# Seven block products for eight in the first FFN products of the last 768 tokens

## The chip, the cores and the metric

The kernel runs on one core of a Trainium2 chip. The metric is the device time of one execution in microseconds (us). One execution was also recorded by the hardware profiler; its own time stands in the table below. Engines are named as the profile names them: PE (TensorE, matmuls), PEld (its weight loads), DVE (VectorE), ACT (ScalarE), POOL (GpSimd), SP (the queue from which all DMAs of this kernel are issued).

## The reference

Attention over 4 batches of 8 heads (576 positions, head size 64) keeps only scores within `tau` of the row's maximum. Its output, 2304 tokens of 512 channels, runs through two feed-forward layers with 2048 hidden channels:

```python
scores = scale * np.matmul(q, k.transpose(0, 1, 3, 2))
thresh = np.max(scores, axis=-1, keepdims=True) - tau
attn   = softmax of the scores that are >= thresh, zero elsewhere
x = (attn @ v) as tokens x channels                      # 2304 x 512
h = x @ w_in;  g = np.maximum(h, 0.0) + alpha * np.minimum(h, 0.0);  x = g @ w_out      # layer 1
h = x @ w_in2; g = h * np.clip(h + 3.0, 0.0, 6.0) / 6.0;             out = g @ w_out2   # layer 2
```

The four weight matrices come as float64. In each FFN product both operands are split into a high and a low float32r part, and three matmuls (high by high, low by high, high by low) make one product.

## The kernel before

**Blocks and weights.** The 2304 tokens are cut into blocks 0 to 3 of 512 tokens (the first 512 positions of each batch) and block 4 of 256 (the last 64 positions of each batch). The hidden channels are 16 tiles of 128, each with one chunk of `w_in` (512 x 128) and one of `w_out` (128 x 512). Block 0's pass decodes each chunk from float64 (`decode`) and writes it to a scratch tensor in DRAM; every later pass loads it from there (`st`, 256 KB) and splits it again into `wi` or `wo` (`split`, L100 to L102: a cast on ACT, a subtraction on POOL or DVE).

**Attention and the queue.** Attention is emitted tile by tile at high priority. `ffn_groups` turns blocks 0 to 2, both layers, into 192 groups: an `h_group` computes one hidden tile (12 matmuls of 512 columns at L216, activation, split of `g`), an `o_group` adds four hidden tiles into one quarter of the output (12 matmuls at L246 or L252). The loop at the end takes groups from this queue between attention tiles at `per` groups a tile; the rest comes after attention.

**The tail.** Blocks 3 and 4 depend on the last attention tiles and run last, layer 1 and then layer 2. For each of 16 hidden tiles and each of the two blocks there are 12 matmuls at L216 (512 columns, then 256), the activation, the split of `g`, and two steps later the output product: L246 in layer 1 (12 of 512 and 12 of 256 columns), L252 in layer 2 (18 of 512 columns). The output sums of a whole layer stay in PSUM.

**What sets the order.** The text of the program, the priorities and a scheduler that simulates the engines fix the order of the instructions on each engine when the program is built. At run time each engine, and SP too, works strictly in that order: a DMA whose operand isn't ready holds every DMA behind it on SP. Tile pools give the buffers; a tile in a reused buffer waits for the last reader of the tile before it.

Of the kernel before, what the change touches and what calls it, by code (L numbers as in the profile page):

```python
# [32 lines left out]
def kernel(  # L33
# [46 lines left out]
    stage = pool(ctx, "stage", 4)  # L80
    gp = pool(ctx, "gp", 5)
    tmp = pool(ctx, "tmp", 2)
    wip = pool(ctx, "wip", 2)
    wop = pool(ctx, "wop", 5)
    dec = pool(ctx, "dec", 3)
    xp = pool(ctx, "xp", 1)
# [493 lines left out]
    x2p = pool(ctx, "x2p", 1, side="right")  # L580
# [5 lines left out]
    ps_h = pool(ctx, "ps_h", 2, space=PSUM)
    ps_o = pool(ctx, "ps_o", 1, space=PSUM)  # L590
    NBR = blocks[B]
    LAGO = 2
    xs = {blk: load_x(x2p.tile([P, 2, NKT, blocks[blk]], F32R, tag=f"x{blk}", name="x"), x1d[blk], blocks[blk], nc.vector)
          for blk in (B - 1, B)}
    for layer in (1, 2):
        c0 = passes.index((layer, None)) * NF
        ready("i", c0)
        oa = [ps_o.tile([P, SM], F32, tag=f"o{d}", name=f"o{d}") for d in range(4)]
        orr = [ps_o.tile([P, SM], F32, tag=f"r{d}", name=f"r{d}") for d in range(2)]
        gss, ys = {}, {}  # L600
        seq = [(ft, blk) for ft in range(NF) for blk in (B - 1, B)]
        for m in range(len(seq) + LAGO):
            if m < len(seq):
                ft, blk = seq[m]
                n = blocks[blk]
                h = ps_h.tile([P, SM], F32, tag="h", name="h")
                mm_h(h, ws["i", c0 + ft], xs[blk], n)
                g = act1(h, ft, n) if layer == 1 else act2(h, ft, n)
                gss[m] = g_hi(g, n)
                g_lo(gss[m], g, n)  # L610
                if blk == B - 1:
                    fetch("i", c0 + ft + 1)
                    ready("o", c0 + ft)
                    ready("i", c0 + ft + 1)
            if m < LAGO:
                continue
            ft, blk = seq[m - LAGO]
            gs = gss.pop(m - LAGO)
            n = blocks[blk]
            first_, last_ = ft == 0, ft == NF - 1  # L620
            if last_ and layer == 1:
                ys[blk] = x2p.tile([P, 2, NKT, n], F32R, tag=f"y{blk}", name="y")
            if layer == 1:
                for d in range(ND):
                    o = oa[d][:, 0:n] if blk < B else orr[d // 2][:, (d % 2) * 256:(d % 2) * 256 + n]
                    mm_o1(o, ws["o", c0 + ft], gs, d, n, first_, last_, fresh=blk < B or d % 2 == 0)
                    if last_:
                        split(ys[blk][:, 0, d], ys[blk][:, 1, d], o, nc.vector)
            else:
                for d in range((n + P - 1) // P):  # L630
                    o = oa[d] if blk < B else orr[d]
                    mm_o2(o, ws["o", c0 + ft], gs, d, n, first_, last_)
                    if last_:
                        t = ob.tile([P, SM], F32, tag="ob", name="ob")
                        w = min(P, n - d * P)
                        if d % 2:
                            nc.vector.tensor_scalar_mul(t[:w], o[:w], 1.0 / 6.0)
                        else:
                            nc.scalar.activation(t[:w], o[:w], AF.Copy, scale=1.0 / 6.0)
                        store(blk, d, t)  # L640
        xs = ys


# [29 lines left out]
```

## Time and profile before

| | us |
|---|---|
| median of three runs (lowest, highest) | 1180.61 (1177.13, 1181.27) |
| the profiled execution, own time | 1179.44 |
| its span, first to last instruction | 1177.7 |
| PE busy in the span | 1125.7 (96%) |
| tail: first matmul of layer 1 on block 3 or 4 to the last matmul | about 892 to 1172 |

The profile gives each engine's busy time, and idle time with what ended it. PE's busy time covers overlapping, modelled matmuls, so the length of one matmul is better taken from the start-to-start distance of a run of them: the chain of waits shows such runs with their start, length and count. A wait on PE costs time; a wait on another engine only if PE waits for it in turn.

### The profile page before, as it was taken

What the parts mean: (1) busy time and instruction counts of PE and PEld (TensorE: products, weight loads), DVE (VectorE), ACT (ScalarE), POOL (GpSimd) and SP (SyncE); (2) the same over time, 40 slices, a digit from 0 to 9 for tenths busy, and PEclk for the clock granted to TensorE, in tenths of its full rate; (3) what the DMA queues carried; (4) which work ended last, traced back from release to release, by engine and by line L of the source; (5) the groups of instructions that cost most, each with busy time, mean ns of one, the idle gap of its engine ahead of it and who ended that gap; (6) DMA issues with size and microseconds to landing.
All of it is one profiled execution on the core that took longest, in us unless ns stands there. A gap on an engine that the chain in (4) does not pass through costs nothing.

```text
span 1177.7 us, 19454 instructions
## 1 busy us (share of the span) xinstructions
PE 1125.7 (96%) x6944; PEld 934.1 (79%) x6944; DVE 649.2 (55%) x1295; ACT 662.6 (56%) x1272; POOL 674.3 (57%) x715
## 2 busy tenths in 40 slices
PE   5799999998999999999999999999999999999998
PEld 4677887777777888888887878887778888888886
DVE  6877798879697545555363537373236333331221
ACT  6887788777787656455655555455434222243332
POOL 2765689887788766555464755545334434334432
PEclk9799999999999999999999999999999999999999
DMA  5743266575766543242424432322235322222211
GB/s 166 218 128 82 80 201 211 152 235 177 230 205 194 149 118 97 76 129 72 124 73 114 137 95 73 103 76 69 83 90 157 86 63 63 63 63 63 64 37 54
DMA packets 92770, 137.51 MB, mean 117 GB/s; under 512 B 19328, under 2 KB 48512, under 8 KB 92672
## 3 DMA queue, kind: packets, MB, share of 16 engines
q1 hardware_dynamic: 92672, 136.26, 39.9%
q8 instruction: 55, 0.90, 0.3%
q14 instruction: 43, 0.35, 0.1%
HBM read 101.72 MB, written 25.17 MB: 108 GB/s over the span
## 4 chain that ended last, share of the span: by engine, by line
PE 71%; ACT 7%; DMA 6%; DVE 6%; issue 4%; POOL 4%; SPq 1%; ACTq 0%; POOLq 0%; DVEq 0%
PE h L216 26%; PE o L246 13%; PE o L252 13%; PE pv L442 5%; PE s L378 5%; PE t L424 3%; DMA st<-wo 2%; PE r L246 2%; PE r L252 2%; PE pt L323 1%; POOL wo L102 1%; DMA wo<-f 1%; ACT f L149 1%; ACT e L400 1%; DVE nmx L399 1%
## 5 line engine op out<-in xcount | busy, mean ns | idle before, releaser
L216 PE MATMUL h<-x,wi 128*128 128x512 f32 (+1 forms) x1536 | 354.4, 379 | 1.1 <-DVE acc L504 0.6
L242 POOL TENSOR_TENSOR gs<-g,gs 128x512 fp32r<-128x512 f32 (+1 forms) x160 | 191.1, 1194 | 216.9 <-ACT gs L238 216.0
L216 PEld LDWEIGHTS h<-x,wi 128*128 128x128 f32 x1536 | 272.3, 188 | 53.4 <-DVE acc L504 1.0
L252 PE MATMUL o<-wo,gs 128*128 128x512 f32 x768 | 195.3, 399 | 8.8 <-DVE g L232 4.7
L246 PE MATMUL o<-gs,wo 128*128 128x512 f32 x768 | 193.5, 397 | 6.2 <-DVE acc L504 2.2
L252 PEld LDWEIGHTS o<-wo,gs 128*128 128x128 f32 x768 | 141.3, 189 | 42.2 <-DVE g L232 7.1
L246 PEld LDWEIGHTS o<-gs,wo 128*128 128x128 f32 x768 | 139.9, 188 | 38.3 <-DVE g L224 5.0
L232 DVE SCALAR_TENSOR_TENSOR g<-m,h 128x512 f32<-128x512 f32 x80 | 50.5, 632 | 163.8 <-ACT m L230 162.3
L221 DVE TENSOR_SCALAR m<-h,alpha_sb 128x512 f32<-128x512 f32 x80 | 55.6, 695 | 148.9 <-PE h L216 148.6
L399 DVE TENSOR_REDUCE nmx<-s 128x1 f32<-128x576 f32 x144 | 107.6, 751 | 37.7 <-PE s L378 37.3
L400 ACT ACTIVATE e<-s,nmx 128x576 f32<-128x576 f32 x144 | 106.9, 747 | 37.4 <-DVE nmx L399 36.8
L238 ACT CAST gs<-g 128x512 fp32r<-128x512 f32 (+1 forms) x160 | 92.8, 580 | 62.3 <-DVE g L224 27.8
L411 POOL TENSOR_SCALAR e<-e,rc 128x576 f32<-128x576 f32 x144 | 109.0, 768 | 29.3 <-DVE rc L408 28.3
L402 DVE SCALAR_TENSOR_TENSOR e<-s,thr,e 128x576 f32<-128x576 f32 x144 | 116.0, 811 | 17.3 <-ACT e L400 14.4
L102 POOL TENSOR_TENSOR wi<-st,wi 128x512 fp32r<-128x512 f32 x56 | 72.9, 1302 | 78.4 <-ACT wi L101 78.2
L442 PE MATMUL pv<-p,v 128*64 128x128 f32 (+1 forms) x1600 | 108.9, 272 | 6.7 <-DVE g L224 2.2
L230 ACT ACTIVATE m<-h,three 128x512 f32<-128x512 f32 x80 | 51.5, 646 | 112.8 <-PE h L216 112.5
L101 ACT CAST wo<-st 128x512 fp32r<-128x512 f32 x96 | 57.1, 619 | 94.1 <-DMA st<-wo 78.2
L442 PEld LDWEIGHTS pv<-p,v 128*64 128x64 f32 x1600 | 84.1, 139 | 29.3 <-issue 16.4
L378 PE MATMUL s<-ka,qt 128*128 128x288 f32 x512 | 100.5, 323 | 6.2 <-DVE thr L401 3.6
L102 POOL TENSOR_TENSOR wo<-st,wo 128x512 fp32r<-128x512 f32 x56 | 74.3, 1343 | 50.9 <-ACT wo L101 50.9
L101 ACT CAST wi<-st 128x512 fp32r<-128x512 f32 x96 | 59.0, 615 | 78.2 <-PE h L216 41.5
(86 smaller groups left out, 1611.8 us busy)
## 6 DMA issues: line engine op xcount, KB each, us to landing
st<-wi SPq DMA_DIRECT2D x96, 256.0 KB, 2.7
st<-wo SPq DMA_DIRECT2D x96, 256.0 KB, 2.7
raw<-in_moe_w_in_dram SPq DMA_DIRECT2D x32, 512.0 KB, 4.6
raw<-in_moe_w_out_dram SPq DMA_DIRECT2D x32, 512.0 KB, 4.2
ka<-ka SPq DMA_DIRECT2D x30, 304.0 KB, 4.3
wi<-f SPq DMA_DIRECT2D x32, 256.0 KB, 3.8
wo<-f SPq DMA_DIRECT2D x32, 256.0 KB, 3.8
raw<-in_k_dram SPq DMA_DIRECT2D x16, 256.0 KB, 3.4
```

The lines of the kernel that those rows point to most:

```text
L101: nc.scalar.copy(hi, src)
L102: lo_eng.tensor_tensor(out=lo, in0=src, in1=f32(hi), op=ALU.subtract)
L216: nc.tensor.matmul(h[:, :n], lhsT=w[:, ws, kt * P:(kt + 1) * P], rhs=x[:, xs, kt, :n], start=(i == 0), stop=(i == len(steps) - 1))
L242: nc.gpsimd.tensor_tensor(out=gs[:, 1, :n], in0=g[:, :n], in1=f32(gs[:, 0, :n]), op=ALU.subtract)
L246: nc.tensor.matmul(o[:, :n], lhsT=w[:, ws, dt * P:(dt + 1) * P], rhs=gs[:, gsel, :n], start=fresh and start and i == 0, stop=stop and i == ...
L252: nc.tensor.matmul(o[:m, :], lhsT=gs[:, gsel, tt * P:tt * P + m], rhs=w[:, ws, :], start=start and i == 0, stop=stop and i == 2)
L378: nc.tensor.matmul(ps[:, half, 0:SH], lhsT=w, rhs=s["k"][:, a, c + half * SH:c + half * SH + SH], start=(n == 0), stop=(n == len(mms) - 1))
L399: nc.vector.tensor_reduce(out=nmx, in_=ps, axis=AX.XY, op=ALU.max, negate=True)
L400: nc.scalar.activation(eh, ps, AF.Exp, bias=nmx, scale=1.0)
L402: nc.vector.scalar_tensor_tensor(out=eh, in0=ps, scalar=thr, in1=eh, op0=ALU.is_ge, op1=ALU.mult, accum_out=sm[:, h:h + 1])
L411: nc.gpsimd.tensor_scalar(out=eh, in0=eh, scalar1=rc[:, h:h + 1], scalar2=0.0, op0=ALU.mult, op1=ALU.add)
L442: nc.tensor.matmul(pv[64 * h:64 * h + 64, :], lhsT=vn[:, h, kt, :], rhs=pt[:, blk, c:c + m], start=(kt == 0), stop=(kt == NB), skip_group_ ...
```

## The change

The tail is written anew. Blocks 3 and 4 are taken as one matrix of 768 tokens. Its product with `w_in` is cut in two along each of its three dimensions: two halves of 384 tokens, two halves of the 512 input channels (256 each), and hidden tile `i` beside hidden tile `i + 8`. Eight block products of 384 columns would make the two hidden tiles; seven make them from sums and differences of the blocks (`half1`, `half2`), at the cost of more additions. The output products keep their number, in another tiling (`o_tile`: 384 columns in layer 1, 512 in layer 2, over four hidden tiles, summed in SBUF).

- **Operands.** Four blocks of x and four differences (T1 to T4; B12 isn't needed itself) are made and split by `x_step`. The seven weight operands of a pair come by DMA, already split (`w_ready`, 1.84 MB, in a `whl` tile): three blocks from `parts`, four sums from `sums`.
- **`parts`.** In block 2's pass each split weight chunk, 64 of 512 KB, is also written to DRAM (in `ready`).
- **`sums`.** `block_sums` makes the four sums of a pair: two loads of 256 KB, four additions of 128x256 on POOL, four splits (ACT cast, POOL subtraction), four writes of 256 KB. Layer 1's eight jobs run between the queue's groups during blocks 1 and 2 (`run_group`); layer 2's eight run in the tail, one for each step of layer 1.
- **Pace.** Eight groups of the queue are kept for after attention (`TAIL`); the first two pairs' products are woven into the last five (`AHEAD`).
- The tail no longer loads and splits `wi` and `wo` chunks; it loads `w_out` split (`wo_ready`, 512 KB).

```diff
@@ ready: every split chunk of block 2 also goes to DRAM
             ws[kind, c] = w
+            if blk == B - 2:
+                nc.sync.dma_start(parts[nm, ft], f32(w))
@@ new
+    def block_sums(layer, i, wf_pool, sh_pool):
+        wf = wf_pool.tile([P, 4, 2 * P], F32, tag="wf", name="wf")
...
+        for out_, in0, in1, op, n in ((a22, a21, a22, ALU.add, 0), (a21, a11, a21, ALU.subtract, 2),
+                                      (a11, a22, a11, ALU.subtract, 1), (a12, a12, a11, ALU.subtract, 3)):
+            nc.gpsimd.tensor_tensor(out=out_, in0=in0, in1=in1, op=op)
+            sh = sh_pool.tile([P, 2, 2 * P], F32R, tag="sh", name="sh")
+            split(sh[:, 0], sh[:, 1], out_, nc.gpsimd)
+            nc.sync.dma_start(sums[layer, i][:, :, 2 * P * n:2 * P * n + 2 * P], f32(sh))
@@ queue
-    per = len(queue) / max(1, NS - PB)
+    jobs = [(1, i) for i in range(NF // 2)]
+    first = len(queue) // (B - 1)
+    every = (len(queue) - TAIL - first) // len(jobs)
...
+    per = (len(queue) - TAIL) / max(1, NS - PB - LAG)
@@ tail, new
+    def w_ready(layer, i):
...
+        w = (whl_q if i % 3 == 2 else whl_p).tile([P, 2, 7, KH], F32R, tag="whl", name="whl")
+        nc.sync.dma_start(f32(w[:, :, 1:3]), parts[f"i{layer}", i].rearrange("p a (b n) -> p a b n", b=2))
+        nc.sync.dma_start(f32(w[:, :, 3:7]), sums[layer, i].rearrange("p a (b n) -> p a b n", b=4))
+        nc.sync.dma_start(f32(w[:, :, 0]), parts[f"i{layer}", i + FH][:, :, KH:])
...
+    def prod(bank, w, x, first):
+        steps = [(ws_, xs_, kt) for ws_, xs_ in ((0, 0), (1, 0), (0, 1)) for kt in range(2)]
+        for n, (ws_, xs_, kt) in enumerate(steps):
+            nc.tensor.matmul(bank[:, 0:TN], lhsT=w[:, ws_, kt * P:kt * P + P], rhs=x[:, xs_, kt, :],
+                             start=first and n == 0, stop=n == len(steps) - 1, skip_group_check=True)
+
+    def half1(i, w, x):
...
+        prod(b1, w["A11"], x["B11"], True)
+        prod(b2, w["S2"], x["T2"], True)
+        prod(b3, w["S1"], x["T1"], True)
...
+        nc.scalar.copy(p1, c1)
+        nc.vector.tensor_tensor(out=u2, in0=c2, in1=p1, op=ALU.add)
+        prod(b1, w["A12"], x["B21"], False)
+        prod(b2, w["S3"], x["T3"], False)
+        nc.vector.tensor_tensor(out=hc[:, 2], in0=c2, in1=p1, op=ALU.add)
+        nc.vector.tensor_tensor(out=hc[:, 2], in0=c3, in1=hc[:, 2], op=ALU.add)
...
+    def half2(i, w, x, made):
+        prod(b2, w["A22"], x["T4"], False)
+        prod(b3, w["S4"], x["B22"], False)
+        nc.vector.tensor_tensor(out=hc[:, 1], in0=b2[:, 0:TN], in1=p1, op=ALU.add)
+        nc.vector.tensor_tensor(out=hc[:, 0], in0=b3[:, 0:TN], in1=u2, op=ALU.add)
...
+    whl_q = pool(rt, "whl3", 1)
+    wo_p = pool(rt, "wo2", 6)
+    gs_p = pool(rt, "gs2", 8)
+    sh_p = pool(rt, "sh2", 2)
```

On PE, in the middle of the tail's layer 1, this stood before (`h` is the first product, `o` and `r` the output sums of blocks 3 and 4):

```order
L216 MATMUL h<-x,wi 128x512 x12
L246 MATMUL o_10493<-gs,wo 128x512 x3
L246 MATMUL o_10494<-gs,wo 128x512 x3
L246 MATMUL o_10495<-gs,wo 128x512 x3
L246 MATMUL o_10496<-gs,wo 128x512 x3
L216 MATMUL h<-x,wi 128x256 x12
L246 MATMUL r_10497<-gs,wo 128x256 x6
L246 MATMUL r_10498<-gs,wo 128x256 x6
```

And this stands there now (`b` is a PSUM bank of block products of one pair, `xT`, `xB` the x operands, `gs` the split activations):

```order
L688 MATMUL b_11728<-xT_10733,whl 128x384 x2
L688 MATMUL b_11729<-xT_10728,whl 128x384 x6
L688 MATMUL b_11727<-xB_10744,whl 128x384 x6
L792 MATMUL o_11767<-gs_11505,wo_11390 128x384 x3
L792 MATMUL o_11767<-gs_11512,wo_11392 128x384 x3
L688 MATMUL b_11852<-xB_10723,whl 128x384 x3
L792 MATMUL o_11781<-gs_11505,wo_11390 128x384 x3
L688 MATMUL b_11728<-xT_10738,whl 128x384 x6
L792 MATMUL o_11781<-gs_11512,wo_11392 128x384 x3
```

The 24 products of one hidden tile have become 42 for a pair of hidden tiles, all of 384 columns, and products of two pairs stand woven with the output tiles of an earlier one.

On SP, at the end of attention, this stood before (`x1d` is the attention output in DRAM, written from `xo`):

```order
L453 DMA x1d_60<-xo 128x512
L169 DMA st<-wo_15_163 128x512
L454 DMA x1d_61<-xo 128x64
L209 DMA st<-x1d_60 128x512 x4
L209 DMA st<-x1d_61 128x256 x4
L169 DMA st<-wi_1_101 128x512
```

And this stands there now (`pi` is a weight chunk's copy in `parts`, `s` a pair's tensor in `sums`):

```order
L484 DMA x1d_60<-xo 128x512
L212 DMA pi_14_149<-wi 128x1024
L175 DMA st<-wi_0_183 128x512
L646 DMA whl<-pi_0_103 128x2x512
L485 DMA x1d_61<-xo 128x64
L647 DMA whl<-s_0_167 128x2x1024
L648 DMA whl<-pi_8_111 128x2x256
L646 DMA whl<-pi_1_104 128x2x512
L647 DMA whl<-s_1_168 128x2x1024
L648 DMA whl<-pi_9_112 128x2x256
L739 DMA xf<-x1d_60 128x4x512
L739 DMA xf<-x1d_61 128x4x256
```

The load of the tail's x (`xf`, 1.57 MB) now stands behind both `whl` tiles of the first two pairs.

On SP, near the end of the tail's layer 1 (nothing of the kind stood there before: a load of `st` for each chunk was all), now:

```order
L646 DMA whl<-pi_1_136 128x2x512
L647 DMA whl<-s_1_176 128x2x1024
L648 DMA whl<-pi_9_144 128x2x256
L234 DMA s_5_180<-sh 256x1x256 x2
L225 DMA wf<-wi_15_230 128x512
L225 DMA wf<-wi_7_222 128x512
L655 DMA wo_11825<-po_7_126 128x1024
L655 DMA wo_11827<-po_15_134 128x1024
L655 DMA wo_12160<-po_0_151 128x1024
```

The `w_out` tiles of layer 1's last pair (`wo_11825`, `wo_11827`) take the buffers of the pair three before, so their loads wait until that pair's last output product is done.

## Rows read from the trace of the kernel before

**Rows 1.** Page, busy time, share of the span and instructions of each engine

```profile
span 1177.7 us, 19454 instructions
PE 1125.7 (96%) x6944; PEld 934.1 (79%) x6944; DVE 649.2 (55%) x1295; ACT 662.6 (56%) x1272; POOL 674.3 (57%) x715
```

**Rows 2.** Windows: stretch, length, busy us by engine, granted TensorE clock, DMA

```profile
core 0: us, PE busy (x) PEld busy (x) DVE busy (x) ACT busy (x) POOL busy (x), PEclk, DMA share, GB/s
130.00:400.00 270.00, 255.34 (x1597) 209.19 (x1598) 224.12 (x434) 210.76 (x393) 223.89 (x228) 0.99 0.63 190
400.00:890.00 490.00, 481.27 (x2977) 396.64 (x2976) 238.19 (x472) 254.20 (x497) 267.35 (x276) 1.00 0.34 97
900.00:1036.00 136.00, 136.00 (x771) 118.94 (x770) 51.15 (x87) 38.27 (x70) 54.10 (x49) 1.00 0.29 81
1037.00:1172.00 135.00, 134.67 (x679) 113.48 (x677) 29.92 (x52) 51.56 (x99) 52.12 (x47) 1.00 0.17 47
```

**Rows 3.** Chain of waits inside the tail's layer 1: start, us, what

```profile
924.42 2.79 PE h L216 x12
927.21 2.75 PE o L246 x12
929.96 1.43 PE h L216 x12
931.38 1.43 PE r L246 x12
932.82 2.79 PE h L216 x12
```

**Rows 4.** Waits on PE from 400 to 890 us: total, times, longest

```profile
PE o L252 <- DVE g L232: 2.5, 6, 0.6
PE pv L442 <- DVE g L224: 2.2, 2, 1.6
```

**Rows 5.** Groups by form, whole span: busy us, mean ns of one, idle before

```profile
L242 POOL TENSOR_TENSOR gs<-g,gs 128x256 fp32r<-128x256 f32 x32 | 24.3, 760 | 36.4 <-ACT gs L238 36.4
L242 POOL TENSOR_TENSOR gs<-g,gs 128x512 fp32r<-128x512 f32 x128 | 166.8, 1303 | 180.5 <-ACT gs L238 179.6
L238 ACT CAST gs<-g 128x256 fp32r<-128x256 f32 x32 | 13.0, 407 | 12.6 <-PE o L252 5.6 <-DVE g L224 5.3 <-DVE g L232 1.1
L238 ACT CAST gs<-g 128x512 fp32r<-128x512 f32 x128 | 79.8, 623 | 49.7 <-DVE g L224 22.4 <-DVE g L232 13.8 <-PE o L252 7.1
L224 DVE SCALAR_TENSOR_TENSOR g<-h,m 128x256 f32<-128x256 f32 x16 | 6.8, 424 | 1.7
L504 DVE TENSOR_TENSOR acc<-o,acc 128x512 f32<-128x512 f32 x36 | 24.4, 683 | 25.6 <-PE o L246 25.6
```

**Rows 6.** Page, DMA issues: count, KB each, median us to landing

```profile
st<-wo SPq DMA_DIRECT2D x96, 256.0 KB, 2.7
raw<-in_moe_w_out_dram SPq DMA_DIRECT2D x32, 512.0 KB, 4.2
x1d<-xo SPq DMA_DIRECT2D x12, 256.0 KB, 3.1
```

**Rows 7.** DMA from 930 to 1030 us: queue, packets, MB, share of 16 engines

```profile
q1 hardware_dynamic: 3456, 6.29, 23.0%
```

**Rows 8.** DMA from 310 to 320 us: GB/s in 40 slices, and queue

```profile
GB/s 160 266 274 344 365 381 401 410 414 406 418 410 418 393 406 362 376 388 379 387 407 328 205 164 115 57 106 78 164 180 229 279 340 393 401 406 393 360 356 385
q1 hardware_dynamic: 2454, 3.15, 93.9%
```

**Rows 9.** Windows, the same columns as Rows 2, around that stretch

```profile
310.00:320.00 10.00, 7.90 (x47) 6.10 (x46) 4.14 (x6) 6.29 (x14) 4.99 (x6) 0.83 0.95 318
```

**Rows 10.** Timeline of PE between attention and tail: start, us, idle before

```profile
882.37 0.80 PE L442 MATMUL pv<-p,v 128*64 128x64 f32 x20
894.62 2.14 PE L216 MATMUL h<-x,wi 128*128 128x512 f32 x8 [0.37 <-ACT x L101]
```

**Rows 11.** Timeline of the last us of the span

```profile
1172.06 0.69 DVE L637 TENSOR_SCALAR ob<-r 128x512 f32<-128x512 f32 x1 [0.52 <-PE r L252]
1172.50 2.52 SPq L534 DMA_DIRECT2D out_dram<-ob  x4
```

More of the change, by code (lines that the diff above doesn't have):

```diff
@@ L62 @@
     LAG = 3
+    TAIL = 8
     OG = 4
@@ L79 @@
     const = pool(ctx, "const", 1)
[L80 to L86, printed above, removed]
+    mid = ExitStack()
+    wip = pool(mid, "wip", 2)
+    stage = pool(mid, "stage", 4)
+    wop = pool(mid, "wop", 5)
+    tmp = pool(mid, "tmp", 2)
+    gp = pool(mid, "gp", 5)
+    xp = pool(mid, "xp", 1)
+    decs = ExitStack()
+    rawp = pool(decs, "rawp", 1)
+    dec = pool(decs, "dec", 3)
     ident = const.tile([P, P], F32, name="ident")
@@ L107 @@
     scratch = {}
+    parts = {(nm, ft): dram.tile([P, 2, DM], F32, name=f"p{nm}_{ft}") for nm in weights for ft in range(NF)}
+    sums = {(layer, i): dram.tile([P, 2, DM * 2], F32, name=f"s{layer}_{i}") for layer in (1, 2) for i in range(NF // 2)}
     if wide:
@@ L204, in ready, with w_src @@
             ws[kind, c] = w
+            if blk == B - 2:
+                nc.sync.dma_start(parts[nm, ft], f32(w))
+    def w_src(nm, ft):
+        if wide:
+            return scratch[nm, ft]
+        return chunk(nm, ft)
+    def block_sums(layer, i, wf_pool, sh_pool):
+        wf = wf_pool.tile([P, 4, 2 * P], F32, tag="wf", name="wf")
+        for slot, ft in ((0, i + NF // 2), (2, i)):
+            src = w_src(f"i{layer}", ft)
+            dst = wf[:, slot:slot + 2]
+            if wide:
+                nc.sync.dma_start(dst.rearrange("p a n -> p (a n)"), src)
+            else:
+                nc.sync.dma_start(dst.rearrange("p a (k f) -> p (a k) f", k=2), src)
+        a21, a22, a11, a12 = [wf[:, s] for s in range(4)]
+        for out_, in0, in1, op, n in ((a22, a21, a22, ALU.add, 0), (a21, a11, a21, ALU.subtract, 2),
[4 more added lines that the diff above has]
+            nc.sync.dma_start(sums[layer, i][:, :, 2 * P * n:2 * P * n + 2 * P], f32(sh))
     def load_x(t, src, n, lo_eng):
@@ L264 @@
     ps_t = pool(psum, "ps_t", 2, space=PSUM)
-    ps_ho = pool(psum, "ps_ho", 2, space=PSUM)
+    ho_bank = ExitStack()
+    ps_ho = pool(ho_bank, "ps_ho", 2, space=PSUM, side="right")
     qr = []
@@ L539, with run_group @@
         queue += ffn_groups(1, b) + ffn_groups(2, b)
-    per = len(queue) / max(1, NS - PB)
+    jobs = [(1, i) for i in range(NF // 2)]
+    first = len(queue) // (B - 1)
+    every = (len(queue) - TAIL - first) // len(jobs)
+    cmb, cmbs = [], ExitStack()
+    def run_group(n):
+        f, a = queue[n]
+        f(*a)
+        if n == first - 1:
+            decs.close()
+            cmb.append(pool(cmbs, "cmb", 2))
+        if n >= first and (n - first) % every == every // 2 and jobs:
+            block_sums(*jobs.pop(0), cmb[0], cmb[0])
+            if not jobs:
+                cmbs.close()
+    per = (len(queue) - TAIL) / max(1, NS - PB - LAG)
+    qs_sb = const.tile([P, 1], F32, name="qs_sb")
+    ntau_sb = const.tile([P, 1], F32, name="ntau_sb")
     x0 = new_x()
@@ L575 @@
         while done < min(len(queue), (i + 1 - PB - LAG) * per):
-            f, a = queue[done]
-            f(*a)
+            run_group(done)
             done += 1
     att.close()
[L580 to L583, printed above, removed]
-    psum.close()
[L589 to L594, printed above, removed]
@@ L595 @@
-    for layer in (1, 2):
[L596 to L622, printed above, removed]
-            if layer == 1:
[L624 to L628, printed above, removed]
-            else:
[L630 to L641, printed above, removed]
@@ new lines @@
+    rt = ExitStack()
+    xop = pool(rt, "xop", 1, side="right")
+    xf_p = pool(rt, "xf", 1, side="right")
+    xt_p = pool(rt, "xt", 2, side="right")
+    whl_p = pool(rt, "whl", 2, side="right")
+    hc_p = pool(rt, "hc", 2, side="right")
+    u_p = pool(rt, "u", 2, side="right")
+    g_p = pool(rt, "g2", 2, side="right")
+    N2 = blocks[B - 1] + blocks[B]
+    TN = N2 // 2
+    FH = NF // 2
+    KH = 2 * P
+    OPS = ("A22", "A11", "A12", "S1", "S2", "S3", "S4")
+    wops, wos = {}, {}
+    def w_ready(layer, i):
+        if i >= FH or (layer, i) in wops:
+            return
+        w = (whl_q if i % 3 == 2 else whl_p).tile([P, 2, 7, KH], F32R, tag="whl", name="whl")
+        nc.sync.dma_start(f32(w[:, :, 1:3]), parts[f"i{layer}", i].rearrange("p a (b n) -> p a b n", b=2))
+        nc.sync.dma_start(f32(w[:, :, 3:7]), sums[layer, i].rearrange("p a (b n) -> p a b n", b=4))
+        nc.sync.dma_start(f32(w[:, :, 0]), parts[f"i{layer}", i + FH][:, :, KH:])
+        wops[layer, i] = {op: w[:, :, n] for n, op in enumerate(OPS)}
@@ new lines, in wo_ready, with x_op, x_diff @@
+    def wo_ready(layer, ft):
+        if (layer, ft) in wos:
+            return
+        w = wo_p.tile([P, 2, DM], F32R, tag="wo2", name="wo2")
+        nc.sync.dma_start(f32(w), parts[f"o{layer}", ft])
+        wos[layer, ft] = w
+    def x_op(xs, nm, src, lo_eng):
+        t = xop.tile([P, 2, 2, TN], F32R, tag=nm, name=f"x{nm}")
+        split(t[:, 0], t[:, 1], src, lo_eng)
+        xs[nm] = t
+    def x_diff(xs, nm, in0, in1, lo_eng):
+        t = xt_p.tile([P, 4 * 2 * P], F32, tag="wf", name="xt")[:, 0:2 * TN].rearrange("p (k n) -> p k n", k=2)
+        nc.vector.tensor_tensor(out=t, in0=in0, in1=in1, op=ALU.subtract)
+        x_op(xs, nm, t, lo_eng)
+        return t
@@ new lines, in x_blocks, with x_step @@
+    def x_blocks(xf):
+        return {f"B{c + 1}{b + 1}": xf[:, 2 * c:2 * c + 2, TN * b:TN * b + TN] for c in range(2) for b in range(2)}
+    def x_step(xs, bl, step):
+        if step == 0:
+            x_op(xs, "B11", bl["B11"], nc.gpsimd)
+        elif step == 1:
+            bl["T1"] = x_diff(xs, "T1", bl["B12"], bl["B11"], nc.vector)
+        elif step == 2:
+            bl["T2"] = x_diff(xs, "T2", bl["B22"], bl["T1"], nc.vector)
+            x_diff(xs, "T3", bl["B22"], bl["B12"], nc.gpsimd)
+            x_op(xs, "B22", bl["B22"], nc.gpsimd)
+        else:
+            x_op(xs, "B21", bl["B21"], nc.vector)
+            x_diff(xs, "T4", bl["B21"], bl["T2"], nc.gpsimd)
@@ new lines @@
+    O1 = [(0, 0), (1, 0), (0, 1), (1, 1), (2, 1), (3, 1), (2, 0), (3, 0)]
+    xf = xf_p.tile([P, ND, N2], F32, tag="xf", name="xf")
+    for blk, at in ((B - 1, 0), (B, blocks[B - 1])):
+        nc.sync.dma_start(xf[:, :, at:at + blocks[blk]], x1d[blk].rearrange("k p n -> p k n"))
+    xs = {}
+    w_ready(1, 0)
+    bl = x_blocks(xf)
+    psum.close()
+    ps_b = pool(rt, "ps_b", 2, space=PSUM)
+    early = {}
+    rest = list(range(done, len(queue)))
+    AHEAD = 5
+    for n in rest[:-AHEAD]:
+        run_group(n)
@@ new lines @@
+    for step in range(4):
+        x_step(xs, bl, step)
+    for n in rest[-AHEAD:]:
+        run_group(n)
+        k = n - rest[-AHEAD]
+        if k == 0:
+            early[0] = half1(0, wops[1, 0], xs)
+        elif k == 1:
+            half2(0, wops[1, 0], xs, early[0])
+            w_ready(1, 1)
+        elif k == 2:
+            early[1] = half1(1, wops[1, 1], xs)
+        elif k == 3:
+            half2(1, wops[1, 1], xs, early[1])
+    ho_bank.close()
+    mid.close()
+    whl_q = pool(rt, "whl3", 1)
```

101 lines of the change are left out of this document (98 added, 3 removed).

## The prediction

> **What bounds the kernel now.** I read the page's busy shares first [rows 1]: PE is busy 96% of the span, no other engine above 57%. Then windows by stage [rows 2]: while block 0's weights are decoded (130 to 400 us) PE loses 15 us of 270 beside DVE and POOL at 83%; from 400 to 890 us it loses 9 of 490; in the tail it is busy 136.0 of 136 us in layer 1 and 134.7 of 135 in layer 2, at a granted clock of 1.00 (the 2.4 GHz level), with DVE, ACT and POOL at 22 to 40%. So the tail, which the change rewrites, lasts as long as its matmuls. The chain of waits there shows nothing else [rows 3]: a hidden tile takes 2.79 + 2.75 + 1.43 + 1.43 = 8.40 us (924.42 to 932.82), sixteen take 134.4, and the layer runs at that pace. Whatever shortens PE's work in the tail shortens the kernel, as long as weights, operands and additions arrive in time.
>
> **The change part by part.**
>
> *The product saved.* [Rows 3]: twelve matmuls of 512 columns start 2.79 us apart from the next group, 232.5 ns each at L216; twelve of 256 columns take 1.43 us, 119.2 ns each; at L246 2.75 us, 229.2 ns, and 1.43. No row shows a matmul of 384 columns; on the line between the two widths it takes 175.9 ns as a first product and 174.2 as an output product. First products before: 16 x (2.79 + 1.43) = 67.5 us a layer. After: 8 pairs x 7 products x 6 matmuls = 336, times 175.9 ns = 59.1 us. Saved 8.4 a layer, 16.8 in both. Output products in layer 1: 384 matmuls on both sides, 66.9 us before and 384 x 174.2 ns = 66.9 after; in layer 2, 288 of 512 columns on both sides. Bounds: with the cost per column of the 256-wide matmul (0.466 ns, 178.8 ns for 384) the first products save 7.5 a layer and layer 1's output products lose 1.8, 13 us in all; with that of the 512-wide one (174.4 and 171.9 ns) it is 19. I take the line between, -16.8, since 384 lies halfway.
>
> The Trainium skill (TensorE: Matmul & The Clock Gate, "Wait — 56ns, not 53.3ns?") gives a warm matmul its columns at 2.4 GHz plus about 2.5 ns. [Rows 3] stand 17 ns above that at 512 columns and 10 ns above at 256, so this case doesn't agree. By the rule 384 columns take 162.5 ns and the saving would be 62.4 - 54.6 = 7.8 us a layer, 15.6 in all; the sum keeps the rows.
>
> *Gone for nothing.* The tail's 64 loads, casts and subtractions of weight chunks go. PE didn't wait for them [rows 2], so they give back no time.
>
> *Added in the middle.* 64 writes of 512 KB (33.6 MB) to `parts` fall into block 2's pass, roughly the second half of 400 to 890 us; the DMA engines carry 97 GB/s there [rows 2] and would carry some 125 more in that half. Layer 1's eight jobs add 8 POOL operations of 128x256 each at 0.76 us, 6.1 us a job, 49 in all, and 32 ACT casts at 0.41, 13 us [rows 5]: POOL goes from 55% to 65% of that stretch. The waits on PE there are 2.5, 2.2 us and less by releaser [rows 4]. Behind a `parts` write, which waits for the chunk's split, stand the next loads on SP; a load lands in 2.7 us [rows 6] and a chunk has the room of a first and an output group (2 x 2.8 us, with attention between) before it is needed. A cast of a sum must wait until the write two before has landed (two buffers), and behind it on ACT stand attention's exponentials. So +2 us, bounds -2 (a new order may also lose some of the 9 us) and +9 (each of the eight jobs costs PE one wait of 1.1 us, the 2.2 in 2 of [rows 4]).
>
> *The entry.* Before, the tail's first matmuls came 12 us after the last attention product at 882.4, and the only wait was 0.37 for the split of x [rows 10]. Now x is loaded behind a `parts` write, a load and both `whl` tiles: 0.52 + 0.26 + 0.30 + 3.67 + 1.57 = 6.3 MB from the end of attention, when the queue's `x1d` write is issued. PE has 36 first and 42 output matmuls between, 36 x 232.5 + 42 x 229.2 ns = 18.0 us. At the 390 GB/s or so that the best slices of [rows 8] hold, 6.3 MB take 16.2 us; at the 318 of that whole stretch 19.9; at the rate implied by the quiet tail, 6.29 MB in 100 us at 23.0%, that is 273 GB/s at 100% [rows 7], 23. With 0.7 for issuing and 0.84 for the first cast of 768 columns ([rows 5], on the line of 256 and 512), the wait is 0, 3.4 or 6.6. I take 2, between the first two. The further operands follow at ACT's and DVE's pace, under 1 us each, against 1.06 us of PE for each product and 24 woven output matmuls: hidden.
>
> *The loop.* A step of layer 1 is 42 x 175.9 + 48 x 174.2 ns = 15.75 us of PE. Beside it stand, from [rows 5] by the same lines: DVE 5 additions, 4 operations of 384, 2 of 768 and 4 output sums, 9.1 us; ACT 3.9; POOL a job's 6.1 and two subtractions of 1.85, 9.8. All fit. The sums in PSUM give waits of their own: `half2` must wait until DVE has read the bank (0.55 us an addition). The order puts other products or output tiles between, 2 us or more. Without that cover it would be 1 to 2 us for each of 16 pairs. I take +2, bounds 0 and 10.
>
> *Between the layers.* `wo_11825` can be loaded once the last output tile of the group before has read the buffer; from there to its first use PE has 21 matmuls, 3.7 us, against 0.3 + 4.2 us for 512 KB [rows 6]: 1 us late. Layer 2's x operands are cast on ACT between the last jobs' casts, each of which waits for a write of 256 KB (3.1 us to land, [rows 6]) and behind it on SP for those `wo` loads; PE has 24 output matmuls and the first products for cover. +2 us, bounds 0 and 6.
>
> *The end.* The last output tile, one sum of 0.69 and a store, as before [rows 11]: the last activation chain, some 9 us, lies beside 19 matmuls and the first halves of the two last tiles. 0.
>
> Sum: 1179.4 (the profiled execution, 1.2 below the median) - 16.8 + 2 + 2 + 2 + 2 = 1170.6; set against the median of 1180.6, 1171.8. Forecast 1172.
>
> **The rivals.**
>
> *The joins eat it (no change).* The mechanism is order: SP, ACT and POOL now carry writes and sums whose turn is fixed, so a late `whl` buffer holds a sums write, that holds a cast on ACT, and that an activation which PE needs. For it: 64 casts wait on writes, where before no cast waited on a store. Against it: PE's own work in front of each such place is 2 to 18 us. At the upper bounds of two of the four joins, middle +9 and entry +6.6 for 2 and 2, it gives 1172 + 11.6 = 1184; at half of that, 1178. I price it at 1181.
>
> *The DMA engines bound layer 1 (slower).* From the end of attention to layer 1's last sums write the queue carries 48.3 MB: 11 `whl` tiles 20.2, 18 `wo` 9.4, 32 sums writes 8.4, 16 loads for them 4.2, the rest 6.1. PE has 24.9 us of queue groups (36 and 72 matmuls) and 126.0 of layer 1, 151 us, so it asks for 320 GB/s. The point is there: below it, layer 2's first weights are late. At 273 GB/s [rows 7] the 48.3 MB take 177 us, 26 late, of which some 5 MB (18 us) may slip into layer 2: 8 to 26, so 1180 to 1198, about 1192. For it: 318 GB/s is all that the fullest stretch moved, at 94% of the engines [rows 8]. Against it: that stretch has slices of 380 to 418 GB/s, and its slow ones hold small packets, while these are 1 to 4 KB. Where PE starved there its granted clock was 0.83 [rows 9], which would add to the price.
>
> The Trainium skill (DMA: Bandwidth & Descriptors, "Where 436 GB/s comes from") holds transfers between HBM and SBUF to about 358 GB/s for a core. [Rows 8] show slices above that, so it isn't a ceiling here; by it the 48 MB take 135 us and hide, which speaks against this rival, though with a tenth to spare.
>
> *The seventh product isn't cheap.* If a matmul of 384 columns costs more than the line, up to 178.8 ns, the forecast moves to 1176; this is inside its range.
>
> **How the numbers follow.** Forecast 1172, own range 1163 to 1178, chance 0.60. Joins eat it, 1178 to 1186: 0.22. DMA bound, above 1186: 0.12. All joins hidden, below 1163 (1180.6 - 19 = 1161.6 at the best): 0.06. A change within 0.5% (1174.7 to 1186.5) is about what a measurement of this kernel can't tell from none. The forecast's upper end beyond 1174.7 holds 0.04, the joins' part faster than that nothing: faster 0.62, same 0.25, slower 0.13 (the last 0.01 from the joins' upper end). The range 1162 to 1187 leaves 0.05 below and 0.12 above.
>
> **What would show it.** Windows over the tail: PE near 100% busy and layer 1 at 126 us, layer 2 at 59 + 66 = 125, against 134.4 each. Matmuls of 384 columns 174 to 179 ns apart in the chain. The last attention product to the first `b` matmul: 18 us if x is in time, else a wait on the `xf` load or the cast behind it. Waits on PE in the middle still under 10 us. DMA share in layer 1 around 0.8; at 0.95 with PE waiting for `whl` or `wo` the second rival is right. Wrong is the forecast if PE waits more than 15 us in the tail, or if the stretch before it grows by more than 10 us.

## The result, and the profile after

| | before | changed |
|---|---|---|
| median of 10 runs each, us (lowest, highest) | 1179.3 (1177.1, 1181.8) | 1187.0 (1181.7, 1194.4) |
| ratio of the times, 95% interval | | 1.0068 [1.0042, 1.0094] |
| profiled execution, own time (span) | 1179.4 (1177.7) | 1192.8 (1191.0) |

Slower by 0.7%, where 1172 was forecast. The changed kernel scatters over 12.7 us, the old one over 4.7; its profiled execution lies 5.8 above its median. The page's busy row, against [rows 1]:

```profile
PE 1119.0 (94%) x6848; PEld 945.0 (79%) x6848; DVE 723.4 (61%) x1359; ACT 658.0 (55%) x1258; POOL 741.4 (62%) x785
```

Windows by stage, columns as in [rows 2]:

```profile
130.00:400.00 270.00, 258.85 (x1631) 212.76 (x1630) 224.60 (x438) 215.34 (x402) 231.02 (x238) 1.00 0.63 195
400.00:890.00 490.00, 468.77 (x2874) 384.90 (x2873) 243.23 (x464) 257.47 (x511) 302.04 (x326) 0.99 0.55 179
...
890.00:1040.00 150.00, 143.07 (x774) 134.13 (x773) 90.97 (x126) 43.24 (x79) 90.40 (x79) 0.99 0.84 297
1040.00:1170.00 130.00, 126.69 (x649) 115.60 (x647) 63.62 (x91) 43.11 (x67) 44.17 (x31) 1.00 0.44 159
```

From 400 to 890 us PE loses 21 us where it lost 9 [rows 2], and in the tail 10 of 280 where it lost almost none. The chain of waits inside the tail's layer 1, against [rows 3]:

```profile
964.68 4.16 PE o L792 x24
968.85 1.91 PE b L688 x11
970.76 4.16 PE o L792 x24
```

A matmul of 384 columns starts every 1.91 / 11 = 174 ns as a block product and 4.16 / 24 = 173 as an output product: the saving is there. Waits on PE from 400 to 895 us, against [rows 4]:

```profile
PE h L246 <- DVE g L254: 5.6, 1, 5.6
PE s L409 <- DVE rc L439: 4.0, 1, 4.0
PE o L276 <- DVE g L254: 2.1, 2, 1.2
```

The three fall between 400 and 510 us. Windows there (same columns), of the changed kernel:

```profile
400.00:420.00 20.00, 15.46 (x88) 12.97 (x87) 13.50 (x29) 7.87 (x16) 19.31 (x26) 0.91 0.74 232
...
460.00:480.00 20.00, 20.00 (x140) 17.02 (x139) 15.45 (x34) 12.25 (x25) 19.67 (x23) 1.00 0.69 214
480.00:500.00 20.00, 14.80 (x90) 12.21 (x88) 13.70 (x19) 9.59 (x21) 18.85 (x25) 0.97 0.30 93
500.00:520.00 20.00, 19.61 (x96) 15.72 (x97) 6.16 (x11) 8.16 (x17) 11.73 (x13) 0.86 0.70 214
```

POOL is busy 17 to 20 us of every 20 from 380 to 500 us: layer 1's eight jobs all run there. Nothing ties a job to its group: its operands come from block 0's scratch alone, so the scheduler could place it long before the group that it follows in the text (tied to their groups, in e3 below, the jobs spread). POOL's order has the 32 sums together, between its 333rd and its 464th instruction of 785. Two places where PE starved, on the timeline:

```profile
401.71 2.50 DVE L106 TENSOR_TENSOR wo<-st,wo 128x512 fp32r<-128x512 f32 x1 [0.46 <-ACT wo L105]
406.74 1.30 PE L409 MATMUL s<-ka,qt 128*128 128x288 f32 x4 [3.99 <-DVE rc L439]
...
493.39 3.75 POOL L106 TENSOR_TENSOR wo<-st,wo 128x512 fp32r<-128x512 f32 x3
493.83 5.90 DVE L106 TENSOR_TENSOR wi<-st,wi 128x512 fp32r<-128x512 f32 x1
498.44 0.75 POOL L106 TENSOR_TENSOR sh<-wf,sh 128x256 fp32r<-128x256 f32 x1
500.39 5.45 PE L246 MATMUL h<-x,wi 128*128 128x512 f32 x12 [5.58 <-DVE g L254]
```

A subtraction on DVE, 0.69 us where nothing holds it, took 5.90 and ended 0.5 us after POOL's run, which stopped at 499.2; `g` came behind it, and PE's twelve matmuls then took 5.45 us and not 2.8, at a granted clock of 0.86 in that window.

**A measure for the middle.** For each of attention's 16 head pairs I take how much later its last product starts than in the kernel before, and add 0.231 us for every queue matmul that is done less by then: the lag. What the span shows beyond the last lag is the tail's doing. The columns name seven of the pairs by the start of their last product in the kernel before, in us; each row is one profiled execution, so differences of 1 or 2 us say little:

| kernel | 313 | 383 | 447 | 510 | 573 | 701 | 883 | tail |
|---|---|---|---|---|---|---|---|---|
| changed | 2.0 | -2.5 | 6.0 | 14.3 | 16.6 | 16.8 | 16.5 | -3.2 |
| no jobs (e1) | 2.1 | -1.7 | -1.3 | 0.2 | 2.5 | 4.1 | 3.6 | -9.2 |
| no writes of `parts` (e2) | 3.2 | -1.0 | 9.0 | 10.7 | 12.9 | 14.6 | 12.7 | 4.6 |
| jobs spread (e3) | -1.0 | -5.6 | -5.2 | -4.6 | 1.6 | 9.8 | 12.1 | -7.6 |
| 16 jobs spread (e6) | 1.8 | -2.5 | -2.1 | 1.8 | 7.1 | 13.1 | 17.0 | -9.4 |
| early loads (e7) | 2.1 | -1.4 | -1.0 | 0.2 | 2.8 | 4.6 | 4.0 | -7.7 |
| single sums (e8) | 2.0 | -2.1 | -1.8 | -1.1 | 1.6 | 3.9 | 3.8 | -3.0 |
| 64 sums, 7 buffers (e9) | 2.8 | -1.3 | -0.9 | 0.6 | 4.9 | 6.9 | 7.8 | -12.4 |
| packed, splits on POOL (e10) | 3.4 | -0.7 | 7.3 | 19.0 | 21.3 | 21.5 | 20.9 | -3.9 |
| 64 sums, 6 buffers (e11) | 1.3 | -2.5 | -2.1 | -0.3 | 4.0 | 6.3 | 8.2 | -8.9 |
| 16 whole jobs, early (e12) | 0.5 | -3.0 | -2.6 | -0.9 | 2.1 | 6.9 | 8.2 | -11.4 |

The changed kernel's span is 13.3 us longer: the middle lost 16.5, nearly all of it while the jobs ran, and the tail gave back 3.2. The tail's longest waits on PE, on the timeline:

```profile
958.33 1.84 PE L792 MATMUL o<-gs,wo 128*128 128x384 f32 x9 [1.37 <-ACT acc L796]
1016.28 1.30 PE L792 MATMUL o<-gs,wo 128*128 128x384 f32 x6 [2.28 <-DMA wo<-po]
1042.75 7.13 PE L792 MATMUL o<-gs,wo 128*128 128x384 f32 x36 [1.58 <-DMA wo<-po]
1081.68 2.18 PE L688 MATMUL b<-xT,whl 128*128 128x384 f32 x11 [1.06 <-DMA whl<-s]
```

These and nine smaller ones make 10.6 us, and around the second the granted clock is 0.91 from 1005 to 1025 us, some 1.8 us more (0.09 x 20). In the same stretch the DMA engines are full, at a share of 1.01 (columns as in [rows 2]):

```profile
1005.00:1025.00 20.00, 17.72 (x93) 17.43 (x92) 8.63 (x15) 4.17 (x10) 11.96 (x13) 0.91 1.01 351
```

### The profile page after: what moved, and what is told of

Same layout as the page of the kernel before. It is cut to its first block, busy times and chain, and to the rows that moved or that the text cites. A ratio compares the mean times of both kernels' runs of the same rounds, so it can differ in the third digit from the quotient of the medians.

```text
span 1191.0 us, 19723 instructions
## 1 busy us (share of the span) xinstructions
PE 1119.0 (94%) x6848; PEld 945.0 (79%) x6848; DVE 723.4 (61%) x1359; ACT 658.0 (55%) x1258; POOL 741.4 (62%) x785
## 4 chain that ended last, share of the span: by engine, by line
PE 51%; DMA 7%; DVE 5%; POOL 4%; issue 3%; ACT 2%; SPq 0%; POOLq 0%; ACTq 0%; DVEq 0%
PE h L246 14%; PE o L282 7%; PE o L276 7%; PE b L688 6%; PE o L794 5%; PE pv L473 3%; PE s L409 3%; PE o L792 3%; PE t L455 2%; DMA st<-wo 1%; DMA s<-sh 1%; DVE g L726 1%; DMA xf<-x1d 1%; DVE xt L665 1%; DMA wo<-po 1%
## 5 line engine op out<-in xcount | busy, mean ns | idle before, releaser
L246 PE MATMUL h<-x,wi 128*128 128x512 f32 x1152 | 289.3, 400 | 8.6 <-DVE g L254 5.6
L246 PEld LDWEIGHTS h<-x,wi 128*128 128x128 f32 x1152 | 213.9, 190 | 58.6 <-DVE g L254 6.0
L272 POOL TENSOR_TENSOR gs<-g,gs 128x512 fp32r<-128x512 f32 x96 | 125.8, 1312 | 86.3 <-ACT gs L268 85.7
L733 POOL TENSOR_TENSOR gs<-g,gs 128x768 fp32r<-128x768 f32 x30 | 56.4, 1880 | 81.2 <-ACT gs L732 71.3
L409 PEld LDWEIGHTS s<-ka,qt 128*128 128x128 f32 x512 | 78.2, 201 | 18.5 <-issue 11.7
L455 PE MATMUL t<-ident,e 128*128 128x128 f32 x576 | 87.8, 279 | 3.5 <-POOL e L442 1.8
L456 ACT COPY p<-t 128x512 f32<-128x512 f32 x144 | 82.2, 595 | 12.1 <-PE t L455 11.5
L160 POOL TENSOR_TENSOR f<-f,low 128x513 uint32<-128x513 uint32 x64 | 76.4, 1194 | 15.9 <-ACT p L456 5.9
L455 PEld LDWEIGHTS t<-ident,e 128*128 128x128 f32 x576 | 67.8, 142 | 16.2 <-POOL e L442 2.9
L688 PE MATMUL b<-xT,whl 128*128 128x384 f32 x384 | 77.8, 340 | 2.9 <-DMA whl<-s 1.1
```

What stands on the lines that cost most here:

```text
L272: nc.gpsimd.tensor_tensor(out=gs[:, 1, :n], in0=g[:, :n], in1=f32(gs[:, 0, :n]), op=ALU.subtract)
L409: nc.tensor.matmul(ps[:, half, 0:SH], lhsT=w, rhs=s["k"][:, a, c + half * SH:c + half * SH + SH], start=(n == 0), stop=(n == len(mms) - 1))
L455: nc.tensor.transpose(ps[:, kt], e[:, c:c + P], ident)
L688: nc.tensor.matmul(bank[:, 0:TN], lhsT=w[:, ws_, kt * P:kt * P + P], rhs=x[:, xs_, kt, :], start=first and n == 0, stop=n == len(steps) - ...
```

## The experiments

Each time stands against the kernel before, run on the same chip.

**No jobs (e1).**

```diff
-            block_sums(*jobs.pop(0), cmb[0], cmb[0])
+            jobs.pop(0)
```

> The changed kernel without layer 1's eight jobs between the queue's groups (the sums of layer 1 are left out; the tail loads as many bytes from `parts` in their place). Theory A (the eight jobs, which ran packed between 380 and 502 us, cost the middle stretch its time: attention came out 11 us later in the profiled run although 2 groups fewer were done by then): the lag at 572 us goes from 16 to under 3 us, the time falls by 8 to 14 us against the changed kernel, to 1173 to 1179. Theory B (the 64 writes of `parts`, with their place on SP and their share of the DMA engines, cost it): the time stays at 1185 to 1189. Theory C (the new pace of groups, 184 groups over fewer attention tiles, costs it): also 1185 to 1189. PE's waits in the tail stay as they are by all three.

1174.6 us, ratio 0.9956 [0.9940, 0.9971]; lag 2.5 at 573 us. Theory A holds: the jobs cost 1187.0 - 1174.6 = 12.4 us. B and C together are left with the 3.6 us of lag that remain. Against expectation the waits in the tail fell too, from 10.6 us in the changed kernel's profiled execution to 5.4; since that execution lies 5.8 above its median, part of this may be its own.

**No writes of `parts` (e2).**

```diff
-            if blk == B - 2:
-                nc.sync.dma_start(parts[nm, ft], f32(w))
```

> The changed kernel without the 64 writes of split weights to `parts` in block 2's pass (left out; the tail loads as many bytes from layer 1's `sums` in their place). Theory A (jobs): within 2 us of the changed kernel, 1185 to 1189, since the lag did not grow from 572 us on, while the writes ran from 635 us. Theory B (writes): 8 us faster, about 1179. Theory C (pace): no change.

1195.9 us, 1.0156 [1.0125, 1.0188]: no theory's number. The middle answers: the lag doesn't grow between 573 and 883 us with the writes (16.6, 16.5) nor without (12.9, 12.7), so they cost nothing there. The loss is in the tail, where the loads now come from another tensor and PE waited up to 5.92 us for one; why they are slower stays open.

**Jobs spread (e3).**

```diff
+        nc.scalar.copy(wf[:, 0:4, 0:1], f32(box["gs"][:, 0, 0:4])...)   # ahead of a job's loads
```

> The changed kernel with each of layer 1's eight jobs held at its own group: a copy of four values of the latest split `g` into the job's buffer stands ahead of its loads, so a job can't run before that group, and the jobs spread from about 400 to 880 us. All work is done. Theory A in the form 'POOL packed without a gap holds others': most of the lag goes, 4 to 10 us faster than the changed kernel, 1177 to 1183, and no subtraction of a weight split on DVE takes over 2 us. Theory A in the form 'POOL and ACT have 62 us more work wherever it stands': within 3 us of the changed kernel. Theory C (pace): no change.

1184.5 us, 1.0051 [1.0033, 1.0070], 2.5 faster than the changed kernel, which is within the second form's 3 us; lag 12.1, which grows from job to job after 510 us. No subtraction on DVE took over 1.64 us, and most of the loss stayed: "packed" alone isn't the cause. The largest of the waits on PE from 400 to 895 us names what took its place:

```profile
PE pt L356 <- ACT p L461: 7.3, 4, 3.1
```

One job on the timeline:

```profile
567.57 1.92 SPq L227 DMA_DIRECT2D wf<-wi  x2
572.63 1.53 POOL L233 TENSOR_TENSOR wf<-wf 128x256 f32<-128x256 f32 x2 [5.50 <-DMA wf<-wi]
573.38 0.40 ACT L105 CAST sh<-wf 128x256 fp32r<-128x256 f32 x1 [4.60 <-POOL wf L233]
574.78 0.27 ACT L461 COPY p<-r 128x128 f32<-128x128 f32 x1
575.10 0.62 PE L356 MATMUL pt<-identr,nat 128*128 128x128 f32 x3 [3.10 <-ACT p L461]
```

The loads are issued at 567.6 and land near 572.6. POOL stands 5.50 us for them at the head of its order, ACT's cast 4.60 behind POOL, attention's `p` behind the cast, and PE 3.10 behind `p`.

**Sixteen jobs spread (e6).** Layer 2's jobs move from the tail to the middle as well.

> As the kernel with the jobs spread, and layer 2's eight jobs also run between the queue's groups (sixteen jobs, one every seven groups), none in the tail. All work is done. If DVE's operations in the tail are stretched by POOL's jobs beside them and SP's jobs there make the w_out loads late: the tail loses 4 to 8 of its 15 us of waits, and POOL in the middle goes from 65 to 75%, which costs 0 to 4: 1172 to 1180. If the tail's waits are of the pairs' own chain and the DMA engines: no gain in the tail, and 1179 to 1186.

1186.9 us, 1.0070 [1.0053, 1.0087]. The middle lost 17.0, 4.9 more than with eight jobs (e3), where the first reading had 0 to 4; the tail gained 9.4, against 7.6 with its jobs (e3): 1.8 more, where it had 4 to 8. The second reading, no gain there, comes nearer.

**Loads one job ahead (e7).**

```diff
+            if held:
+                sums_make(*jobs[m // every - 1], held.pop(0), cmb[0], anchor=True)
+            held.append(sums_load(*jobs[m // every], cmb[0], True))
```

> The kernel with the jobs spread, but a job's two loads are issued one job ahead (15 groups of the queue, some 55 us, before its sums; an operation of one column on DVE that reads the latest split `g` holds the sums at their own place). All work is done. In the trace of the spread jobs POOL stood up to 5.50 us for `wf<-wi`, with ACT's cast of the sum 4.60 behind it and attention's `p` behind that, and PE waited 7.3 us for `p`. Theory D (a job costs through its late load, which holds POOL and ACT in their order): the waits for `p` go, the lag of attention falls from 12.6 to 3 to 6 us, 1174 to 1179. Theory E (62 us more of POOL and ACT cost it wherever they stand): no change against the spread jobs, 1182 to 1187.

1176.5 us, 0.9985 [0.9974, 0.9996]; lag 4.0, as without any job (3.6). The same wait on PE, from 400 to 895 us:

```profile
PE pt L368 <- ACT p L473: 1.2, 2, 0.7
```

Theory D holds, E falls: the same sums, casts and writes cost 12.4 us in one arrangement and about 2 in the other (1176.5 against 1174.6 without them).

**Single sums spread (e8).** The four sums of a job at four places.

> As the kernel with early loads, but each job is cut into its four sums, each held at a place of its own, one every 3.5 groups of the queue (some 13 us), so that POOL never has more than 1.5 us of it at a time. All work is done. Theory D (late loads alone): the same as with early loads, within 2 us. Theory F (a job's 6 us on POOL and ACT at one place are too much even with the data there): 2 to 5 us faster than with early loads, near 1174.5, the time without the jobs. Theory E (the work costs wherever it stands): 1182 to 1187 again.

1180.2 us, 1.0013 [0.9992, 1.0033], from 1173.8 to 1188.2: 3.7 above e7, where D had at most 2. In the middle it is as e7 (lag 3.8), so F falls. The profiled execution, which lies at the median, has 11.1 us of waits in the tail (e7 6.9); that the scatter comes from there too isn't shown.

**64 sums in the middle, seven `w_out` buffers (e9).**

```diff
-    wo_p = pool(rt, "wo2", 6)
-    sh_p = pool(rt, "sh2", 2)
+    wo_p = pool(rt, "wo2", 7)
```

> As the kernel with single sums spread, with layer 2's eight jobs there too (64 sums, one every 1.75 groups), none in the tail, and a seventh buffer for the w_out tiles of the tail, which takes the memory that the tail's jobs had. All work is done. If the tail's wait of about 2 us for `wo<-po` between the layers, with 1.5 to 2 us of half-speed matmuls behind it, comes from the buffer: it shrinks to under 1 us, and the tail is 3 us shorter. By theories D and F the 32 further sums cost the middle 0 to 4 us: 1168 to 1176 in all. By theory E they cost another 10: 1190 or more.

1174.9 us, 0.9962 [0.9947, 0.9976]: faster than both kernels. POOL is busy 359 of 490 us there, 73%, with a lag of 7.8; at 62% the changed kernel's was 16.5. The tail gains 12.4.

**DVE beside POOL (m1).**

> A kernel that only measures: DVE's operations of 128x512 alone and beside an unbroken run of subtractions on POOL (16 of 128x512, then 24 of 128x256), for three kinds on DVE: both operands in SBUF, one in PSUM and one in SBUF, one operand in SBUF. None of the reference is computed. If POOL's unbroken work holds DVE's operations with two operands in SBUF: alone 0.69 us, beside POOL some take 2 us and more, until POOL's run ends or pauses; with an operand in PSUM or a single operand they keep to 0.7 us. If the 5.90 us in the changed kernel had another cause (a semaphore, the clock of DVE): all three kinds keep to 0.7 us beside POOL.

DVE's operations by line (ns, shortest/median/longest): both operands in SBUF, one in PSUM, one operand in SBUF:

```profile
L80 DVE TENSOR_TENSOR dout<-din,dhi x40: 684/1205/1751, 6.5 to 56.1; 128x512 f32<-128x512 f32 x40
```

```profile
L84 DVE TENSOR_TENSOR dout<-acc,dhi x40: 677/680/692, 64.1 to 99.1; 128x512 f32<-128x512 f32 x40
```

```profile
L88 DVE TENSOR_SCALAR dout<-din x40: 418/942/1485, 107.2 to 146.1; 128x512 f32<-128x512 f32 x40
```

With PSUM nothing is held. With two SBUF operands it is, up to 1.75 us, and against expectation with one as well. The Trainium skill (SBUF — State Buffer, "SBUF: two separate sides") has an exclusive lock between GpSimd and DVE operations with two SBUF inputs or in a two-port mode, held for one whole instruction. For two SBUF inputs this trace agrees: 0.68 us alone, 1.20 to 1.75 beside POOL. In which mode the operation with one ran, no run shows.

**A single operation that comes to a running POOL (m2).**

> A kernel that only measures, none of the reference is computed: DVE runs one, three or six additions with an operand in PSUM and then one subtraction with two operands in SBUF, over and over, beside an unbroken run of subtractions on POOL (24 of 128x512; then 512 and 256 mixed). In the first measurement each such operation of DVE took at most 1.75 us, as long as itself and one operation of POOL. If a single one that comes to a running POOL is held until POOL pauses: some take 5 us and more, up to the whole of POOL's run (29 us). If it is held for one operation of POOL at most: none over 2 us, and the 5.90 us in the changed kernel has a further cause that stays open.

```profile
L84 DVE TENSOR_TENSOR wt<-din,wt x46: 674/1147/1228, 11.6 to 187.8; 128x512 fp32r<-128x512 f32 x46
```

None over 1.23 us: held for part of one POOL operation. The 5.90 us lasted through six of POOL's, from a cause that stays open. In the other kernels' traces the longest such operation from 130 to 890 us is 2.60, in e2, which packs its jobs too, and 1.85 in the rest.

**Packed, DVE's splits on POOL (e10).**

```diff
-                on_dve = ft % 4 < (1 if layer == 1 and blk is not None else 2)
+                on_dve = blk != 1 and ft % 4 < (1 if layer == 1 and blk is not None else 2)
```

> The changed kernel, jobs packed as in it, but no subtraction of a weight split runs on DVE while block 1's pass lasts: all go to POOL (some 24 of 1.3 us more there, a third of them beside the jobs), so that DVE has hardly an operation with two SBUF operands left that POOL could hold. All work is done. Theory G (the packed jobs cost mainly because DVE's subtractions are held, one for 5.90 us, and `g` behind them): the lag at 572 us falls from 16 to 6 to 10 us, 1179 to 1184. Theory H (they cost because POOL is full, 92% of 120 us, and all that waits in its order is late): the lag grows by 3 to 10 us, 1188 to 1197.

1196.8 us, 1.0145 [1.0121, 1.0170]; lag 21.3 at 573 us, 4.7 more. Theory H holds, G falls. Two windows:

```profile
400.00:420.00 20.00, 16.75 (x100) 13.71 (x99) 10.87 (x28) 8.77 (x19) 19.49 (x25) 1.00 0.75 237
...
440.00:460.00 20.00, 15.00 (x85) 11.14 (x84) 1.44 (x2) 6.84 (x17) 16.67 (x21) 0.83 0.62 194
```

**Six buffers again (e11).** Against e9 one number changes.

> As the kernel with all 64 sums spread in the middle and seven w_out buffers in the tail (1174.9), with six buffers again; nothing else differs. If the late `wo<-po` between the layers comes from the buffers: the wait goes from 0.80 back to 1.6 to 2.4 us, the granted clock behind it from 1.00 to 0.91 over 20 us (1.8 us), the time 2 to 4 us up, to 1177 to 1179. If it was the tail's jobs in SP's order that made it late: no change, 1174 to 1176.

1178.9 us, 0.9997 [0.9983, 1.0011], 4 above e9, from 1175.7 to 1184.2. But the wait for `wo<-po` is 0.76 us here and 0.80 in e9: in this execution the buffer isn't what made them differ. With the tail's jobs gone the wait was 1.80 in e6, so SP's order isn't all of it either. What sets it stays open. Of the 3.9 us between the two profiled spans, 1.6 are the clock (last section) and 1.0 longer waits in the tail.

**Sixteen whole jobs, early (e12).**

> As that kernel with seven buffers, but each of the sixteen jobs makes its four sums at one place, with loads one job ahead (7 groups, some 27 us), and not one sum at a time. If single sums are the better form for POOL (1.5 us at a time, not 6): 2 to 5 us slower, 1177 to 1180. If only the loads' landing decides, as between the early loads and the single sums in the eight jobs, whose lag was 3.3 and 4.4 us: the same within 2 us, 1173 to 1177.

1175.7 us, 0.9967 [0.9955, 0.9979], as e9 within the noise, with a lag of 8.2 against 7.8: whether POOL takes 1.5 or 6 us at a time makes no difference that these runs can tell, and that the loads have landed (e7 against e3) does.

## Why the prediction was wrong

- **The middle, +2 with bounds -2 and 9: the step that failed.** "POOL goes from 55% to 65% of that stretch" spread the jobs over 490 us, as the text of the program does. The order had them in 120 us, with POOL 93% busy. Measured: 12.4 us, by e1; the prediction's own sign of being wrong, 10 us more before the tail, came true with 16.5 of lag. The upper bound priced eight waits of 1.1 us, from waits of a POOL that was half idle; behind a full one attention's normalisation, the splits and `g` all come late at once (e10: 24 more operations of 1.3 us on it, a third of them beside the jobs, made the lag 4.7 us larger and the time 9.8; where the other 5 lie isn't shown).
- **The casts that wait for a write of sums, named in that +2.** They were there, but don't decide: from 375 to 895 us ACT waited 14.7 us before such casts in the changed kernel and 23.8 in e12, whose lag is half as large with twice the jobs.
- **The writes of `parts`, part of that +2.** Right: no lag while they run (e2).
- **The product, -16.8.** Right: 174 and 173 ns against 175.9 and 174.2.
- **The entry, +2.** Right: the first block product starts at 912.2, 18.1 us after attention's last product ended, and the waits from there up to 926 make 1.5 us.
- **The loop and between the layers, +2 each.** Too small in the profiled execution: listed waits after 940 us are 9.1 us, and the clock around one of them takes 1.8: 11 for 4. In e1 the whole tail lists 5.4. The unforeseen part is `wo` late twice, 2.28 and 1.58; the prediction had one, 1 us. Its price of a landing came from a quiet queue, 4.2 us for 512 KB [rows 6]; from 890 to 1040 us it is 7.6, with the DMA engines 83% busy:

```profile
q1 hardware_dynamic: 22842, 44.42, 83.3%
...
wo<-po SPq DMA_DIRECT2D x18, 512.0 KB, 7.6
```

- **The rivals.** The time lies just above the range of "The joins eat it" and just inside that of "The DMA engines bound layer 1", which is luck for the second. The first had the right kind of cause, work whose turn is fixed, in the wrong place: it looked for a late `whl` buffer that holds a write, a cast and an activation in the tail. The second needs a share of 0.95 over layer 1; 0.83 and 4.9 us of waits for DMA say no, although it holds from 1005 to 1025 us. One of its arguments was misread: the slow slices of [rows 8] don't hold smaller packets. From 315 to 318 us they are 1.26 KB on average, at 193 GB/s with the engines 67% busy; from 318 to 320 they are 1.09 KB, at 379 GB/s.

Without the jobs (e1) the kernel gains 4.3 us where the other terms promised 10.8: 3.6 of the difference is the lag that is left without them, 1.6 a tail that gains 9.2 for 10.8, and the rest lies between the profiled execution and the median. So about 12 of the 15 us between forecast and result are the jobs, and 10.5 of them (1187.0 - 1176.5, e7) their arrangement. In the packed order POOL waited only 0.3 us for a job's loads from 380 to 502 us, so the late loads of e3 are a second way to lose the time and not the cause of the first; there it is the full POOL, as far as e10 shows.

## What to carry to other kernels

Work put on an engine with room on average must be read in the order of instructions before its share is divided by a stretch: ready work is hoisted and packs. Tie such work to its place by a cheap dependence, and give its loads a lead of several times their landing time (20 to 38 us were enough in e12, for loads that landed in 5 in e3); otherwise an in-order engine stands at the head of its queue for a load, and the next engines behind it.

## What the runs showed of the hardware

The same wait, at the same place, may or may not cost the clock. PE's timeline and windows in e9:

```profile
938.27 1.33 PE L711 MATMUL b<-xT,whl 128*128 128x384 f32 x6 [1.35 <-DVE hc L726]
939.43 1.23 PE L711 MATMUL b<-xB,whl 128*128 128x384 f32 x6
```

```profile
940.00:945.00 5.00, 5.00 (x30) 5.00 (x29) 4.79 (x8) 1.22 (x3) 2.39 (x2) 1.00 1.04 400
```

and in e11:

```profile
938.61 2.18 PE L711 MATMUL b<-xT,whl 128*128 128x384 f32 x6 [1.36 <-DVE hc L726]
940.58 1.94 PE L711 MATMUL b<-xB,whl 128*128 128x384 f32 x6
```

```profile
940.00:945.00 5.00, 5.00 (x25) 5.00 (x24) 3.56 (x5) 1.31 (x2) 2.71 (x2) 0.78 1.06 400
```

After 1.35 us of idling PE went on at 2.4 GHz; after 1.36, for a while at 1.2 GHz, which took 1.6 us more. In both, PE had done the same products in the 10 us before, and idled 0.39 us once. That such waits are why the changed kernel scatters more than the old one is a guess; no run shows it.
